# Moving weight sums down VectorE's queue, and using the seven-product form one chunk earlier

## The chip, the cores and the metric

The kernel runs on one core of a Trainium2 chip. The metric is the device time of one execution in microseconds (us); lower is better. The profile of one execution is shown beside the times; its span is about 1.8 us shorter than the time.

Engine names in the profile: PE is TensorE, PEld its weight loads, DVE is VectorE, ACT is ScalarE, POOL is GpSimd (here it only issues loads), SP issues stores.

## The reference, cut to what matters

Attention with projected keys and values, followed by a feed-forward layer with a squared ReLU. There are 8 batches of 1024 tokens, 8 heads of 64.

```python
k_proj = np.einsum('ks,bhsd->bhkd', E, k)         # 64 projected keys per head
v_proj = np.einsum('ks,bhsd->bhkd', F, v)
scores = scale * np.matmul(q, k_proj.transpose(0, 1, 3, 2))
attn = softmax(scores)                            # cut
x = (attn @ v_proj), heads joined: 8192 x 512     # cut
h = np.maximum(x @ w_in, 0.0)                     # 512 -> 2048, the first layer
out = h * h @ w_out                               # 2048 -> 512, the second layer
```

## The kernel before

Each batch is worked in two chunks of 512 tokens. A chunk first does the first layer (16 blocks `fb` of four 512-column products, ReLU on ScalarE into `h_relu`, square on VectorE into `hsq`), then the second layer. The attention of the next batch is put between these steps by a plan: `at(step, ...)` issues a piece behind that step. TensorE's order is as written. The order on the other engines is chosen by a scheduler at build time, and each of them then works strictly in that order.

The second layer of a chunk has two forms. The plain form is 64 products of 512 columns. The other uses seven half-size matrix products in place of eight (112 of 256 columns) and needs eight sums of quarters of `w_out` (once, into `w_sum`) and eight sums of quarters of `hsq` (per chunk, `h_sum`, with one written over `hsq`), all on VectorE.

```python
def sum_w_out():                                  # 8 instructions on VectorE
    for j in range(2):
        ...                                       # quarters of w_out_sb[j], w_out_sb[j + 2]
        for o, x, y in ((t1, b12, b11), (t3, b22, b12), (t2, b22, t1), (t4, b21, t2)):
            nc.vector.tensor_tensor(out=o, in0=x, in1=y, op=ALU.subtract)

def seven_products(self, c):                      # cut
    first, chain, other = bank(), bank(), bank()
    half(c, 1, 0, first, True); yield             # needs the squares of fb 0 to 7
    half(c, 1, 1, first, True)
    nc.scalar.copy(chain[:], first[:]); yield     # ScalarE: starts the chain of product 6
    half(c, 5, 0, other, True); yield             # needs the first h sums
    half(c, 5, 1, other, True); yield
    half(c, 6, 0, chain, False); yield            # ...

def steps(self):                                  # cut
    for c in range(2):
        seven = self.b > 0                        # the first batch uses the plain form
        order = [fb for j in range(HF) for fb in (j, HF + j)] if seven else range(fb0, NFB)
        for n, fb in enumerate(order):
            ...                                   # 4 products, ReLU, square; h sums after n = 7 and 15
            yield

# the plan of the first batch (b == 0), cut
at(1, att.project_v, V_PIECES[1])                 # its own attention still runs in chunk 0
at(2, att.chunk_values, 0, 1, (0,))
at(36, nxt.project)                               # the next batch's attention, in chunk 1
at(39, nxt.transpose_k)
at(45, nxt.sums, 0)
at(48, nxt.values, 0, True)                       # True: into banks of the first layer
at(48, nxt.scores, 2)
...
at(64, sum_w_out)                                 # last in the program
```

PSUM is in two pools: `bank()` turns round four banks used by both layers, and `att_psum()` round two tiles for the attention. Of the attention's tiles, `vp` holds the projected values, `rs` the inverse row sums (VectorE copies part of them to other partitions: the `rs` copies), and `xT` the attention's result, which is the first layer's input.

The softmax here doesn't subtract the row's maximum and nothing guards it: scores larger than these inputs give would overflow.

Of the kernel before, what the change touches and what calls it, by code (L numbers as in the profile page):

```python
# [18 lines left out]
def kernel(  # L19
# [11 lines left out]
    nc = tc.nc  # L31
# [41 lines left out]
    def bank(shape=(P, 512), dtype=F32):  # L73
        return fps.tile(list(shape), dtype, tag="bank", name="ps_bank")
# [61 lines left out]

    w_sum = wpool.tile([P, 4, HF, HM], BF16, name="w_sum")

    def sum_w_out():
        for j in range(2):  # L140
            f = slice(j * fn, (j + 1) * fn)
            t1, t2, t3, t4 = (w_sum[:, n, f] for n in range(4))
            up, down = w_out_sb[j], w_out_sb[j + 2]
            b11, b12, b21, b22 = up[:, :, 0:HM], up[:, :, HM:DM], down[:, :, 0:HM], down[:, :, HM:DM]
            for o, x, y in ((t1, b12, b11), (t3, b22, b12), (t2, b22, t1), (t4, b21, t2)):
                nc.vector.tensor_tensor(out=o, in0=x, in1=y, op=ALU.subtract)
# [34 lines left out]
    class Attention:  # L181
# [58 lines left out]
        def transpose_k(self, gs=(0, 1)):  # L240
            ps = bank([P, H // 2, 2, KP], BF16)
            rows = slice((LO, HI)[gs[0]].start, (LO, HI)[gs[-1]].stop)
            g = slice(gs[0], gs[-1] + 1)
            for j in range(H // 2):
                nc.tensor.transpose(
                    ps[:, j, g, :].rearrange("p g k -> p (g k)"),
                    self.kp[rows, j].rearrange("k a d -> k (a d)"), ident[rows, rows]
                )
            nc.vector.tensor_copy(self.kT[:, :, g], ps[:, :, g])

        def transpose_k_dma(self):
            nc.sync.dma_start_transpose(
# [122 lines left out]
    class Ffn:  # L375
# [113 lines left out]
        def steps(self):  # L489
            for c in range(2):  # L490
                self.hsq[c] = hsq_pool.tile([P, 2, 2, HF, HC], BF16, name="hsq")
                seven = self.b > 0
                if seven:
                    self.h_sum = form_pool.tile([P, 3, HF, HC], BF16, name="h_sum")
                first = self.cold and c == 0
                fb0 = 0
                if first:

                    banks = [bank() for _ in range(4)]
                    for cbs, fbs in (  # L500
                        ((0, 1), (0, 1)), ((0, 1), (2, 3)), ((2,), (0, 1)), ((2,), (2, 3)), ((3,), (0, 1, 2, 3)),
                    ):
                        for fb in fbs:
                            for cb in cbs:
                                self.first_mm(c, fb, cb, banks[fb])
                            if cbs[-1] == NCB - 1:
                                self.square(c, fb, banks[fb])
                        if (cbs, fbs) != ((2,), (2, 3)):
                            yield
                    fb0 = 4  # L510
                order = [fb for j in range(HF) for fb in (j, HF + j)] if seven else range(fb0, NFB)
                for n, fb in enumerate(order):
                    ps = bank()
                    for cb in range(NCB):
                        self.first_mm(c, fb, cb, ps)
                    self.square(c, fb, ps)
                    if seven and n % HF == HF - 1:
                        self.sum_h(c, slice(n // HF * HF // 2, (n // HF + 1) * HF // 2))
                    yield
                if first:  # L520

                    for t0 in range(0, 4, 2):
                        banks = [bank() for _ in range(2)]
                        for j in range(WP):
                            for t in range(2):
                                for fb in range(j * fn, (j + 1) * fn):
                                    self.second_mm(c, t0 + t, fb, banks[t])
                                if j == WP - 1:
                                    self.store(c, t0 + t, banks[t])
                                yield  # L530
                elif seven:
                    yield from self.seven_products(c)
                else:
                    for tb in range(4):
                        ps = bank()
                        for j in range(WP):
                            for fb in range(j * fn, (j + 1) * fn):
                                self.second_mm(c, tb, fb, ps)
                            if j == WP - 1:
                                self.store(c, tb, ps)  # L540
                            yield

    with tc.manual_schedule(engines={PE}):
# [28 lines left out]
        coming = None  # L572
        for b in range(B):
            plan = {}

            def at(step, fn, *args, **kwargs):
                plan.setdefault(step, []).append(lambda: fn(*args, **kwargs))

            if b == 0:
                at(1, att.project_v, V_PIECES[1])  # L580
                at(2, att.chunk_values, 0, 1, (0,))
                at(2, att.project_v, V_PIECES[2])
                at(3, att.chunk_values, 0, 1, (1,))
                at(21, att.transpose_q_chunk, 1, Q0, 0)
                at(21, att.transpose_q_chunk, 1, Q0, 1)
                at(23, att.chunk_scores, 1, 0)
                at(23, att.chunk_scores, 1, 1)
                at(25, att.sums, 0)
                at(27, att.chunk_values, 1, 0)
                at(27, att.chunk_values, 1, 1)  # L590
                nxt = Attention(1)
                nxt.load()
            if b + 1 < B:
                if b + 2 < B:
                    coming = Attention(b + 2)
                    coming.load()
                if b == 0:
                    at(36, nxt.project)
                    at(39, nxt.transpose_q, 0)
                    at(39, nxt.transpose_q, 1)  # L600
                    at(39, nxt.transpose_k)
                    at(41, nxt.scores, 0)
                    at(41, nxt.scores, 1)
                    at(44, nxt.transpose_q, 2)
                    at(44, nxt.transpose_q, 3)
                    at(45, nxt.sums, 0)
                    at(48, nxt.values, 0, True)
                    at(48, nxt.scores, 2)
                    at(51, nxt.values, 1)
                    at(51, nxt.scores, 3)  # L610
                    at(55, nxt.sums, 2)
                    at(55, nxt.values, 2)
                    at(55, nxt.values, 3, True)
                else:
                    at(14, nxt.scores, 0)
                    at(14, nxt.scores, 1)
                    at(18, nxt.sums, 0)
                    at(18, nxt.values, 0)
                    at(21, nxt.scores, 2)
                    at(26, nxt.values, 1)  # L620
                    at(26, nxt.scores, 3)
                    at(48, nxt.sums, 2)
                    at(48, nxt.values, 2)
                    at(51, nxt.values, 3)
                if b + 2 < B:
                    if b == 0:
                        at(61, coming.project)
                        at(63, coming.transpose_q_dma)
                        at(64, coming.transpose_k)
                        at(64, sum_w_out)  # L630
                    else:
                        at(26, coming.project)
                        at(30, coming.transpose_q_dma)
                        at(28, coming.transpose_k_dma)
            for step, _ in enumerate(Ffn(att, b == 0).steps(), 1):
                for stage in plan.pop(step, []):
                    stage()
            assert not plan, plan
            att, nxt = nxt, coming
# [30 lines left out]
```

## Time and profile before

| | before |
|---|---|
| time | 512.07 us (511.62 to 512.73, 3 runs) |
| span of the profile | 510.1 us |
| TensorE busy | 96% of the span |
| VectorE / ScalarE busy | 60% / 55% |

From the second batch on TensorE works almost without a gap. The first batch does not. These are TensorE's longest waits in the kernel before (who waited, for what: us in all, times, longest):

```profile
PE ps_att L296 <- DVE vp L238: 12.4, 2, 11.2
PE ps_bank L471 <- DVE xT L371: 2.0, 3, 1.5
PE ps_bank L410 <- DVE hsq L386: 1.9, 6, 0.3
```

`vp` is the copy of projected values out of PSUM. The copy itself is short, so the question is what it stood behind. This is TensorE's timeline before, from 19 us (start, duration, engine, line, operation; in brackets the idle time in front of it and what ended it):

```profile
20.23 0.64 PE L235 MATMUL ps_att<-V_sb,FT 128*64 128x128 bf16 x16
20.80 1.04 PE L471 MATMUL ps_bank<-xT,w_in 128*128 128x512 bf16 x4
33.08 0.43 PE L296 MATMUL ps_att<-expT,vp 64*64 64x256 bf16 x4 [11.24 <-DVE vp L238]
...
38.49 13.93 PE L471 MATMUL ps_bank<-xT,w_in 128*128 128x512 bf16 x54
52.25 1.03 PE L477 MATMUL ps_bank<-w_out,hsq 128*128 128x512 bf16 x4
```

And VectorE's timeline in the same stretch:

```profile
18.75 0.68 DVE L371 TENSOR_TENSOR xT<-ps_att,rs 128x512 bf16<-128x512 f32 x1
32.13 0.69 DVE L146 TENSOR_TENSOR w_sum<-w_out 128x1024 bf16<-128x1024 bf16 x1 [12.69 <-DMA w_out<-in_moe_w_out_dram]
32.74 0.28 DVE L238 CAST vp<-ps_att 128x128 bf16<-128x128 f32 x1
34.63 0.69 DVE L146 TENSOR_TENSOR w_sum<-w_out 128x1024 bf16<-128x1024 bf16 x1 [1.61 <-DMA w_out<-in_moe_w_out_dram]
35.24 0.68 DVE L371 TENSOR_TENSOR xT<-ps_att,rs 128x512 bf16<-128x512 f32 x1
```

Read the two together. The projection that `vp` copies had ended by 20.9 us, yet the copy ran at 32.74. In front of it stood a sum of `w_out`, whose data landed only at about 32.1. The sum is written last in the program and is not needed before the second batch, but the scheduler placed it here. The Trainium skill (TensorE: Matmul & The Clock Gate, "Architectural detail") says that VectorE's and ScalarE's queues are strict FIFO while TensorE's can only pull weight loads ahead; this trace agrees: nothing overtook the waiting sum for 12.69 us.

The page's strip of the granted TensorE clock (40 slices of 12.75 us, in tenths) shows a second cost:

```profile
PEclk9958999999999999999999999999999999999999
```

The granted clock was 0.51 from 25.5 to 38 us and 0.50 from 38 to 42 us, so the 54 products at 38.49 took longer than the 11.7 us that 54 times 0.216 us make.

### The profile page before, as it was taken

The numbers are of one execution on the slowest core, as the hardware profiler recorded it, in microseconds if no ns is written. First come the engines' busy times: TensorE is split into PE (matmuls) and PEld (weight loads), VectorE is DVE, ScalarE is ACT, GpSimd is POOL, SyncE is SP. The second block draws the span as 40 slices with busy tenths as digits, with TensorE's granted clock in tenths as the row PEclk, the third lists the DMA queues.
The fourth block names the chain that finished last, engine by engine and source line by source line (L and its number), as shares of the span: only waits on it lengthen the run. The fifth ranks groups of instructions, "written<-read, shape, count | busy, mean of one in ns | idle before, by whom it ended". The sixth has DMA issues, their size and how long they took to land.

```text
span 510.1 us, 8489 instructions
## 1 busy us (share of the span) xinstructions
PE 487.1 (96%) x3434; PEld 287.8 (56%) x3434; DVE 304.9 (60%) x586; ACT 282.7 (55%) x425; POOL 32.5 (6%) x45
## 2 busy tenths in 40 slices
PE   8629999999999999999999999999999999999996
PEld 4214444445657465665748465574747566575755
DVE  2226266667666675857667665756767574757271
ACT  2306447547464775647465675747665575745351
POOL 7420010010100002000100000000000000000000
PEclk9958999999999999999999999999999999999999
DMA  9999999994697009920499106020330202020202
GB/s 174 204 204 207 208 209 181 198 202 81 136 192 158 21 1 220 203 83 1 93 172 198 47 1 175 2 84 0 91 86 1 82 2 84 0 84 1 82 2 84
DMA packets 74905, 54.30 MB, mean 106 GB/s; under 512 B 29169, under 2 KB 73457, under 8 KB 74865
## 3 DMA queue, kind: packets, MB, share of 16 engines
q0 software_dynamic: 30640, 29.23, 36.1%
q1 hardware_dynamic: 44224, 24.52, 18.3%
q8 instruction: 27, 0.44, 0.3%
q14 instruction: 14, 0.11, 0.1%
HBM read 59.24 MB, written 16.78 MB: 149 GB/s over the span
## 4 chain that ended last, share of the span: by engine, by line
PE 86%; DMA 6%; issue 3%; ACT 3%; DVE 1%; POOL 1%; POOLq 0%
PE ps_bank L471 41%; PE ps_bank L410 33%; PE ps_bank L477 4%; DMA w_out<-in_moe_w_out_dram 3%; DMA V_sb<-in_v_dram 3%; PE ps_bank L215 2%; PE ps_att L342 2%; ACT h_relu L384 1%; PE ps_att L320 1%; PE ps_att L286 1%; ACT expT L300 1%; DVE hsq L386 1%; DVE xT L371 0%; PE ps_bank L271 0%; POOL K_sb L80 0%
## 5 line engine op out<-in xcount | busy, mean ns | idle before, releaser
L471 PE MATMUL ps_bank<-xT,w_in 128*128 128x512 bf16 x1024 | 228.8, 382 | 2.1 <-DVE xT L371 2.0
L384 ACT ACTIVATE h_relu<-ps_bank 128x512 bf16<-128x512 f32 x256 | 151.8, 599 | 107.9 <-PE ps_bank L471 107.7
L471 PEld LDWEIGHTS <-w_in 128*128 128x128 bf16 x1024 | 99.6, 98 | 122.8 <-issue 9.7
L386 DVE TENSOR_TENSOR hsq<-h_relu 128x512 bf16<-128x512 bf16 x256 | 105.8, 423 | 90.0 <-ACT h_relu L384 89.1
L410 PEld LDWEIGHTS <-hsq 128*128 128x128 bf16 x896 | 86.6, 98 | 19.0 <-DVE hsq L386 3.6
L410 PEld LDWEIGHTS <-h_sum 128*128 128x128 bf16 x672 | 63.8, 98 | 12.5 <-issue 5.5
L410 PE MATMUL ps_bank<-w_out,hsq 128*128 128x256 bf16 x448 | 56.8, 273 | 1.9 <-DVE hsq L386 1.9
L410 PE MATMUL ps_bank<-w_sum,hsq 128*128 128x256 bf16 x448 | 53.5, 273 | 0.0
L410 PE MATMUL ps_bank<-w_sum,h_sum 128*128 128x256 bf16 x448 | 53.4, 273 | 0.0
L330 DVE COPY rs<-rs 32x1024 f32<-32x1024 f32 x60 | 41.1, 685 | 20.3 <-ACT rs L325 19.4
L420 DVE TENSOR_TENSOR o_sb<-ps_bank,u 128x512 f32<-128x512 f32 x28 | 19.4, 691 | 46.9 <-PE ps_bank L410 30.4
L428 ACT COPY u<-ps_bank 128x512 f32<-128x512 f32 x28 | 16.4, 585 | 39.9 <-PE ps_bank L410 39.9
L300 ACT ACTIVATE expT<-ps_att 128x1024 bf16<-128x1024 f32 x32 | 31.9, 1025 | 2.7 <-PE ps_att L286 2.6
L346 DVE TENSOR_TENSOR xT<-ps_att,rs 128x512 bf16<-128x512 f32 x52 | 33.0, 685 | 0.5
L477 PE MATMUL ps_bank<-w_out,hsq 128*128 128x512 bf16 x128 | 29.2, 380 | 0.0
L410 PE MATMUL ps_bank<-w_out,h_sum 128*128 128x256 bf16 x224 | 26.7, 273 | 0.0
L418 ACT COPY o_sb<-ps_bank 128x512 f32<-128x512 f32 x28 | 16.4, 585 | 14.3 <-PE ps_bank L410 14.1
L477 PEld LDWEIGHTS <-hsq 128*128 128x128 bf16 x128 | 11.9, 98 | 15.5 <-issue 1.9
L398 DVE TENSOR_TENSOR h_sum<-hsq 128x1024 bf16<-128x1024 bf16 x28 | 19.4, 692 | 1.0
L398 DVE TENSOR_TENSOR h_sum<-h_sum,hsq 128x1024 bf16<-128x1024 bf16 x28 | 19.3, 689 | 0.5
L398 DVE TENSOR_TENSOR h_sum<-hsq,h_sum 128x1024 bf16<-128x1024 bf16 x28 | 19.2, 684 | 0.0
L398 DVE TENSOR_TENSOR hsq<-hsq 128x1024 bf16<-128x1024 bf16 x28 | 19.2, 684 | 0.0
(71 smaller groups left out, 256.0 us busy)
## 6 DMA issues: line engine op xcount, KB each, us to landing
out_dram<-o_sb SPq DMA_DIRECT2D x64, 256.0 KB, 2.3
K_sb<-in_k_dram POOLq DMA_DIRECT2D x7, 1024.0 KB, 14.2
V_sb<-in_v_dram POOLq DMA_DIRECT2D x7, 1024.0 KB, 19.4
Q_sb<-in_q_dram POOLq DMA_DIRECT2D x7, 1024.0 KB, 15.2
w_out<-in_moe_w_out_dram POOLq DMA_DIRECT2D x4, 512.0 KB, 17.0
w_in<-in_moe_w_in_dram POOLq DMA_DIRECT2D x3, 512.0 KB, 14.7
k_f<-in_k_dram SPq DMA_DIRECT2D x1, 512.0 KB, 4.3
Q_sb<-in_q_dram POOLq DMA_DIRECT2D x2, 256.0 KB, 7.8
```

The costliest lines, as they stand in the source:

```text
L300: nc.scalar.activation(e[:], ps[:], AF.Exp, scale=SCALE)
L330: nc.vector.tensor_copy(rs[j][lack:lack + 32], rs[j][have:have + 32])
L346: nc.vector.tensor_tensor(out=self.xT[:, pr, :, par], in0=ps_x[par].rearrange("p (c t) -> p c t", c=2), in1=rs[:, par].rearrange("p (c t) ...
L384: nc.scalar.activation(r[:], ps[:], AF.Relu)
L386: nc.vector.tensor_tensor(out=self.hsq[c][:, fb // HF, :, fb % HF, :], in0=rv, in1=rv, op=ALU.mult)
L398: nc.vector.tensor_tensor(out=o, in0=x, in1=y, op=op)
L410: nc.tensor.matmul(ps[:, i * HM:(i + 1) * HM], lhsT=h[:, fb, i * P:(i + 1) * P], rhs=w_out_form(n, fb), start=fresh and i == 0 and fb == 0 ...
L418: nc.scalar.copy(o[:], ps[:])
L420: nc.vector.tensor_tensor(out=o[:], in0=ps[:], in1=more[:], op=ALU.add)
L428: nc.scalar.copy(u[:], ps[:])
L471: nc.tensor.matmul(ps[:], lhsT=w_in_blk(cb, fb), rhs=self.xT[:, cb, c].rearrange("p a t -> p (a t)"), start=(cb == 0), stop=(cb == NCB - 1),)
L477: nc.tensor.matmul(ps[:, m], lhsT=self.quarter(c, fb // HF, tb // 2)[:, fb % HF, (tb % 2) * P:(tb % 2 + 1) * P], rhs=w_out_blk(fb)[:, m], ...
```

## The change

Its intent has three parts: queue the sums of `w_out` later on VectorE; with the sums in hand, use the seven products in the first batch's second chunk too; and in batches 1 to 6 put the next batch's row sums and values ahead of the seven products. `tc.issue_after(x)` makes the scheduler queue what stands inside it behind instruction `x`; here that is the copy of the next batch's `kT`.

```diff
-    def sum_w_out():
+    def sum_w_out(behind):
+        with tc.issue_after(behind.queued.ins):
+            sum_w_out_now()
+
+    def sum_w_out_now():
...
-            nc.vector.tensor_copy(self.kT[:, :, g], ps[:, :, g])
+            self.queued = nc.vector.tensor_copy(self.kT[:, :, g], ps[:, :, g])
...
-                seven = self.b > 0
+                seven = self.b > 0 or c > 0
...                                                # first batch
+                    at(46, sum_w_out, nxt)
-                    at(55, nxt.values, 3, True)
+                    at(57, nxt.values, 3)
...                                                # later batches
-                    at(14, nxt.scores, 0)          # and scores 1
-                    at(18, nxt.sums, 0)            # and values 0
-                    at(21, nxt.scores, 2)
+                    at(12, nxt.scores, 0)
+                    at(16, nxt.sums, 0)
+                    at(20, nxt.scores, 2)
-                    at(48, nxt.sums, 2)            # and values 2
-                    at(51, nxt.values, 3)
+                    at(46, nxt.sums, 2)
+                    at(50, nxt.values, 3)
...                                                # first batch: 62 steps now, not 64
-                        at(61, coming.project)
-                        at(63, coming.transpose_q_dma)
-                        at(64, coming.transpose_k)
-                        at(64, sum_w_out)
+                        at(59, coming.project)
+                        at(61, coming.transpose_q_dma)
+                        at(62, coming.transpose_k)
```

(The last hunks are shortened; `and ...` comments stand for lines that move alike.)

More of the change, by code (lines that the diff above doesn't have):

```diff
@@ L612 @@
                     at(55, nxt.values, 2)
-                    at(55, nxt.values, 3, True)
+                    at(57, nxt.values, 3)
                 else:
-                    at(14, nxt.scores, 0)
-                    at(14, nxt.scores, 1)
-                    at(18, nxt.sums, 0)
-                    at(18, nxt.values, 0)
-                    at(21, nxt.scores, 2)
+                    at(12, nxt.scores, 0)
+                    at(12, nxt.scores, 1)
+                    at(16, nxt.sums, 0)
+                    at(16, nxt.values, 0)
+                    at(20, nxt.scores, 2)
                     at(26, nxt.values, 1)
                     at(26, nxt.scores, 3)
-                    at(48, nxt.sums, 2)
-                    at(48, nxt.values, 2)
-                    at(51, nxt.values, 3)
+                    at(46, nxt.sums, 2)
+                    at(46, nxt.values, 2)
+                    at(50, nxt.values, 3)
                 if b + 2 < B:
                     if b == 0:
-                        at(61, coming.project)
-                        at(63, coming.transpose_q_dma)
-                        at(64, coming.transpose_k)
-                        at(64, sum_w_out)
+                        at(59, coming.project)
+                        at(61, coming.transpose_q_dma)
+                        at(62, coming.transpose_k)
                     else:
```

## The prediction

> **What bounds the kernel.** TensorE: busy 96% of a 510.1 us span; from the second batch on a batch takes 58.0 us, 57.7 of them TensorE (table by stage). Its waits lie in the first 40 us: the waits view has 12.4 us for VectorE's `vp` copy, 11.2 in one wait. The timeline: VectorE's queue is in order, and a `vp` copy of a product that ended near 20.9 us runs at 32.74, behind a sum of `w_out` that waited 12.69 us for the first `w_out` piece. The next copies wait for pieces landing near 34.6 and 37.2 us. Then the granted clock is 0.51 (25.5 to 38 us) and 0.50 (38 to 42). The Trainium skill (TensorE: Matmul & The Clock Gate, Part 1) says an idle window halves the clock; the trace agrees.
>
> **Sums moved.** `vp` is then copied near 21 us. The waits of the DMA queue put the last V piece at 22.1 us and `w_in` pieces at 24.7, 27.2, 29.8: in time. 54 products at 0.216 us put the first second-layer product at about 36 us instead of 52.25. `w_out` lands at 32.1, 34.6, 37.2 and 42.4 us, just ahead of use. Gain: 16 us, 2 of them clock. The next batch's K, V and Q (landed by about 53 and 58 us) stay ahead of their use at about 57 and 61.
>
> **Seven products in the first batch's second chunk.** 64 products of 512 columns at 0.2225 us (14.2 us) become 112 of 256 at 0.109 (12.25): 2.0 us less.
>
> **Added there on VectorE.** Eight sums of `w_out` and eight of `h`, 0.61 us each: 9.8 us, on 24.8 us busy in 37.5. In the changed order all eight sums of `w_out`, four `h` sums and four `rs` copies (0.7 us) stand before the fifteenth square, which the first of the seven products needs. Summed from the `kT` copy (79.49 us in the old trace), it ends near 93.5; TensorE wants it at 89.6: 4 us of wait, 0.7 more for the second `h` sums, and 1 us at the last product, whose bank waits for an output sum behind the late `xT` products. I expect 5.7 us of new wait: the stage gets 3.7 us longer, not 2 shorter.
>
> **Sums and values ahead of the products (batches 1 to 6).** They fill the wait for the last squares (1.9 us in six waits). ScalarE now does Ln and two Exp (3.2 us) before the copy that starts the third product's chain; it should end about when TensorE comes (0 to 0.3 us per chunk). Net 1.5 us gained.
>
> **Sum.** 512.1 - 16.0 - 2.0 + 5.7 - 1.5 = 498.3 us; 8 in 10 between 493.5 and 502.5. Faster by over 2% (under 501.8): 0.87; within 2%: 0.12; slower: 0.01.
>
> **Right if:** no wait for `vp` over 1 us, clock 1.0 between 20 and 52 us, first second-layer product near 36 us, next projection near 57. In the first batch's second chunk waits of TensorE for `hsq`, `h_sum` or `xT` of 3 to 8 us, VectorE over 85% busy there. 112 more 256-wide products, 64 fewer 512-wide. Later batches: no wait for `hsq`, 57.7 us each.
>
> **Wrong if:** loads land later once TensorE is early (a DMA wait near 22, 42 or 57 us); less waiting in the second chunk (down to 492 us), or more, with a clock that falls again (up to 505); ScalarE's chain copy late in all twelve later chunks (up to 7 us).

## The result

The changed kernel takes 499.27 us (498.89 to 499.96, 4 runs); the kernel before, with the run beside it, 512.32 us. The ratio is 0.9748 (95% interval 0.9731 to 0.9765). All outputs are right. Ratios here are the mean time of one kernel's fast runs over that of the other's of the same rounds, so they are not quite the ratio of the medians quoted.

TensorE's waits after (lines of the changed kernel are four higher, so L414 is the old L410):

```profile
PE ps_bank L414 <- DVE hsq L390: 3.6, 1, 3.6
...
PE ps_bank L475 <- DVE xT L375: 1.1, 4, 0.3
...
PE ps_bank L414 <- DVE o_sb L424: 0.5, 1, 0.5
PE ps_bank L414 <- ACT u L432: 0.3, 1, 0.3
```

The wait for `vp` is gone, and so are the six waits for `hsq` of the later batches; one new wait of 3.6 us has come. TensorE's timeline after, the start of the first batch:

```profile
21.78 0.64 PE L239 MATMUL ps_att<-V_sb,FT 128*64 128x128 bf16 x16
22.35 1.04 PE L475 MATMUL ps_bank<-xT,w_in 128*128 128x512 bf16 x4
23.32 0.30 PE L300 MATMUL ps_att<-expT,vp 64*64 64x256 bf16 x4
...
26.11 11.58 PE L475 MATMUL ps_bank<-xT,w_in 128*128 128x512 bf16 x51 [0.26 <-DVE xT L375]
37.53 4.48 PE L481 MATMUL ps_bank<-w_out,hsq 128*128 128x512 bf16 x20
```

VectorE's timeline after, in the same stretch:

```profile
22.46 0.29 DVE L242 CAST vp<-ps_att 128x128 bf16<-128x128 f32 x1 [1.47 <-PE ps_att L239]
23.74 0.69 DVE L375 TENSOR_TENSOR xT<-ps_att,rs 128x512 bf16<-128x512 f32 x1 [0.99 <-PE ps_att L300]
24.35 0.28 DVE L242 CAST vp<-ps_att 128x128 bf16<-128x128 f32 x1
```

The `vp` copy now runs as soon as its product has ended, the products of the values follow at once, and the second layer starts at 37.53 us in place of 52.25. The granted clock was 1.00 from 20 to 52 us. In the page's strip (slices of 12.45 us here) the first 8 lies before this stretch, and the second, in the seventh slice, belongs to the new wait:

```profile
PEclk8999998999999999999999999999999999999999
```

Now the same kernel's timeline where the new wait is, the start of the seven products in the first batch's second chunk:

```profile
74.07 0.94 PE L414 MATMUL ps_bank<-w_out,hsq 128*128 128x256 bf16 x7
78.65 1.67 PE L414 MATMUL ps_bank<-w_out,hsq 128*128 128x256 bf16 x9 [3.65 <-DVE hsq L390]
80.19 1.87 PE L414 MATMUL ps_bank<-w_sum,h_sum 128*128 128x256 bf16 x8
```

Seven products run, using the squares of `fb` 0 to 6; the eighth needs `fb` 7, the fifteenth square in this order. VectorE's timeline shows what it stood behind:

```profile
72.52 0.68 DVE L150 TENSOR_TENSOR w_sum<-w_out,w_sum 128x1024 bf16<-128x1024 bf16 x1
73.12 0.68 DVE L150 TENSOR_TENSOR w_sum<-w_out 128x1024 bf16<-128x1024 bf16 x1
73.72 0.42 DVE L390 TENSOR_TENSOR hsq<-h_relu 128x512 bf16<-128x512 bf16 x1
74.06 0.68 DVE L150 TENSOR_TENSOR w_sum<-w_out,w_out 128x1024 bf16<-128x1024 bf16 x1
74.75 2.78 DVE L334 COPY rs<-rs 32x1024 f32<-32x1024 f32 x4
77.56 0.69 DVE L150 TENSOR_TENSOR w_sum<-w_out,w_sum 128x1024 bf16<-128x1024 bf16 x1
78.17 0.42 DVE L390 TENSOR_TENSOR hsq<-h_relu 128x512 bf16<-128x512 bf16 x1
```

No line has an idle time: VectorE is working through a backlog. The square that TensorE waits for is the one at 78.17.

The stages of both kernels, in us, from the timelines (a boundary is the first product of a layer):

| stage | before | after | difference |
|---|---|---|---|
| start to the first product of the first layer | 18.89 | 20.44 | +1.55 |
| first batch, chunk 0, first layer | 33.36 | 17.09 | -16.27 |
| first batch, chunk 0, second layer | 16.67 | 16.66 | 0 |
| first batch, chunk 1 | 37.53 | 42.76 | +5.23 |
| batches 1 to 6 | 347.41 | 344.63 | -2.78 |
| batch 7 | 56.24 | 56.21 | -0.03 |
| span | 510.1 | 497.8 | -12.3 |

The trace of the changed kernel lacks some matmul records (992 of the first layer's 1024 are there), among them the first product of batches 2 to 7. The table puts these starts one product (0.22 us) before the first record; the complete traces of other runs with the moved steps give the same 344.6 us.

The first row is not the change's: over twelve profiles that stage took 18.59 to 21.46 us, with no relation to the kernel (the same source gave 20.44 and 18.66). The kernel before absorbs a late start in its wait and the changed kernel does not, so the first two rows belong together: -14.7 us (worked out below). A profile's span is therefore a poor measure of 1 us; the timed runs decide there.

### The profile page after: what moved, and what is told of

The parts are those of the page before. It is cut to its first block, busy times and chain, and to the rows that moved or that the text cites. A ratio compares the mean times of both kernels' runs of the same rounds, so it can differ in the third digit from the quotient of the medians.

```text
span 497.8 us, 8559 instructions
## 1 busy us (share of the span) xinstructions
PE 482.8 (97%) x3446; PEld 293.4 (59%) x3482; DVE 310.9 (62%) x596; ACT 281.6 (57%) x426; POOL 32.5 (7%) x45
## 4 chain that ended last, share of the span: by engine, by line
PE 89%; DVE 6%; ACT 2%; issue 1%; DMA 1%; DVEq 0%; POOLq 0%
PE ps_bank L475 42%; PE ps_bank L414 37%; PE ps_bank L219 2%; PE ps_att L346 2%; PE ps_att L290 2%; DMA K_sb<-in_k_dram 1%; DVE rs L334 1%; PE ps_bank L481 1%; DVE xT L375 1%; PE ps_att L324 1%; DVE w_sum L150 1%; DVE hsq L390 1%; PE ps_bank L228 1%; PE ps_bank L179 1%; DVE qT L279 1%
## 5 line engine op out<-in xcount | busy, mean ns | idle before, releaser
L475 PE MATMUL ps_bank<-xT,w_in 128*128 128x512 bf16 x992 | 223.3, 379 | 3.0 <-DVE xT L375 1.1
L414 PEld LDWEIGHTS <-hsq 128*128 128x128 bf16 x960 | 92.1, 98 | 22.1 <-issue 6.9
L414 PEld LDWEIGHTS <-h_sum 128*128 128x128 bf16 x720 | 69.8, 98 | 12.4 <-issue 4.1
L414 PE MATMUL ps_bank<-w_out,hsq 128*128 128x256 bf16 x480 | 60.6, 274 | 3.6 <-DVE hsq L390 3.6
L414 PE MATMUL ps_bank<-w_sum,h_sum 128*128 128x256 bf16 x480 | 57.9, 275 | 0.0
L414 PE MATMUL ps_bank<-w_sum,hsq 128*128 128x256 bf16 x480 | 57.5, 272 | 0.3 <-ACT u L432 0.3
L424 DVE TENSOR_TENSOR o_sb<-ps_bank,u 128x512 f32<-128x512 f32 x30 | 20.7, 691 | 55.9 <-PE ps_bank L414 30.9
L414 PE MATMUL ps_bank<-w_out,h_sum 128*128 128x256 bf16 x240 | 28.6, 273 | 0.5 <-DVE o_sb L424 0.5
L80 POOL DMA_DIRECT2D K_sb<-in_k_dram x9 | 7.8, 861 | 138.5 <-PE ps_bank L220 134.1
L330 ACT ACTIVATE rs<-rs 128x1024 f32<-128x1024 f32 x15 | 15.9, 1062 | 0.5
## 6 DMA issues: line engine op xcount, KB each, us to landing
w_out<-in_moe_w_out_dram POOLq DMA_DIRECT2D x4, 512.0 KB, 17.8
w_in<-in_moe_w_in_dram POOLq DMA_DIRECT2D x3, 512.0 KB, 14.7
k_f<-in_k_dram SPq DMA_DIRECT2D x1, 512.0 KB, 4.3
```

Of the source, the lines that this page charges most:

```text
L330: nc.scalar.activation(rs[1][:], rs[1][:], AF.Exp, scale=-1.0)
L414: nc.tensor.matmul(ps[:, i * HM:(i + 1) * HM], lhsT=h[:, fb, i * P:(i + 1) * P], rhs=w_out_form(n, fb), start=fresh and i == 0 and fb == 0 ...
L424: nc.vector.tensor_tensor(out=o[:], in0=ps[:], in1=more[:], op=ALU.add)
L475: nc.tensor.matmul(ps[:], lhsT=w_in_blk(cb, fb), rhs=self.xT[:, cb, c].rearrange("p a t -> p (a t)"), start=(cb == 0), stop=(cb == NCB - 1),)
```

## The experiments

All ran with rounds of the kernel before on the same chip, whose medians were 511.6 to 512.0 us. My theory had three parts: (1) the early sums, by holding VectorE's queue, were the whole of the first gap; (2) the sums standing among the squares make the new wait; (3) the moved steps shorten the later batches. The rivals were that the seven products carry part of the gain, that the `h` sums and not the sums of `w_out` make the new wait, and that batches 1 to 6 are shorter for another reason.

### One part at a time

**Sums of `w_out` only** (`e1_sums_only`): the two hunks of `sum_w_out` and `self.queued`, `at(46, sum_w_out, nxt)`, and nothing else.

```diff
-    def sum_w_out():
+    def sum_w_out(behind):
+        with tc.issue_after(behind.queued.ins):
...
+                    at(46, sum_w_out, nxt)
...
-                        at(64, sum_w_out)
```

> Only the sums of w_out move on VectorE (queued as in the changed kernel); no seven products in the first batch's second chunk, no step moves. Theory (the early sums hold VectorE's queue, and nothing else was needed): the first second-layer product starts 16.3 us earlier than before, and the second chunk of the first batch keeps its 37.5 us, because without the products' sums the late squares are still in time: 496.0 us, so faster than the changed kernel (499.3). Rival (the seven products are part of the gain, and the wait in the second chunk comes from the sums of w_out alone): a wait of some 4 us stays in the second chunk and the time is 500 to 503 us.

Measured: 496.74 us (496.08 to 496.87), ratio 0.9708 (0.9691 to 0.9724). Chunk 0's first layer fell to 17.08 us and chunk 1 kept its 37.54; the second layer began at 37.18 us, so 15.1 us earlier and not 16.3 (why is said under the first gap below). The theory holds, and one part of the change alone beats the whole.

**Seven products only** (`e2_seven_only`): the sums stay where the scheduler put them. By my notes, a first build read `w_sum` before it was written, since the sums stood behind their use in the program; it was never run. The run has `at(46, sum_w_out)` instead, and its trace shows the scheduler still hoisting the sums to the front (the first at 32.19 us).

```diff
-                seven = self.b > 0
+                seven = self.b > 0 or c > 0
...
+                    at(46, sum_w_out)
...                                                # and the first batch's steps 57, 59, 61, 62
```

> Only the seven products in the first batch's second chunk (with that batch's own step numbers, which the shorter chunk forces); the sums of w_out stay early in VectorE's queue. The 12.4 us of waits for vp must stay. Theory: TensorE has 2.0 us less to do there, and the h sums alone make it wait about 1.7 us (fifteenth square 0.5, second h sums 1.2): 511.5 to 512.5 us, the second chunk 37.2 us long instead of 37.5. Rival (the wait of 3.65 us comes from the h sums or the rs copies, not from the sums of w_out): the chunk gets as long as in the changed kernel, 42.8 us, and the time is 517 us.

Measured: 513.81 us (513.41 to 514.79), ratio 1.0049 (1.0034 to 1.0064): slower than before, a small but clear difference. Chunk 1 took 39.86 us, so 2.7 us more than I expected and 2.9 less than in the changed kernel. Neither side was right: the sums of `w_out` cost about 2.9 us of the 42.8, and the seven products lose on their own.

**Steps of batches 1 to 6 only** (`e3_steps_only`):

```diff
-                    at(18, nxt.sums, 0)            # and 14, 21, 48, 51, as in the change
+                    at(16, nxt.sums, 0)            # and 12, 20, 46, 50
```

> Only the moved steps of batches 1 to 6 (sums and values ahead of the products). Theory: each of these batches gets 0.46 us shorter (58.21 to 57.75), 2.8 us in all: 509.5 us. Rival (the shorter batches of the changed kernel have another cause, such as the loads being further ahead): no change, 512.3 us.

Measured: 509.29 us (508.98 to 509.46), ratio 0.9957 (0.9942 to 0.9972). Batches 1 to 6 took 344.64 us in place of 347.40. The theory holds. The start of the seven products in batch 1, in the kernel before and in this run:

```profile
120.93 0.93 PE L410 MATMUL ps_bank<-w_out,hsq 128*128 128x256 bf16 x7
122.17 1.16 PE L410 MATMUL ps_bank<-w_out,hsq 128*128 128x256 bf16 x9 [0.32 <-DVE hsq L386]
```

```profile
121.95 1.92 PE L410 MATMUL ps_bank<-w_out,hsq 128*128 128x256 bf16 x16
```

The row sums and values stand before the products now, and the sixteen run without a break.

### The sums where VectorE is idle

**Sums in the gap** (`e4_sums_in_gap`): VectorE was idle for 5.95 us in chunk 0's second layer, after the `qT` copies, and all of `w_out` has landed by then.

```diff
-            nc.vector.tensor_copy(self.qT[:, 4 * hg:4 * hg + 4, 2 * c:2 * c + 2, :], ps[:])
+            self.queued = nc.vector.tensor_copy(self.qT[:, 4 * hg:4 * hg + 4, 2 * c:2 * c + 2, :], ps[:])
...
-                    at(46, sum_w_out, nxt)
+                at(21, sum_w_out, att)
```

> The changed kernel with the sums of w_out queued behind the two qT copies of the first batch's chunk 1, where VectorE was idle for 5.95 us (43.8 to 49.7 us in the changed kernel); eight sums take 4.9 us. Theory (the wait of 3.65 us, the half clock after it and the two small waits come from the sums standing among the squares): the second chunk of the first batch falls from 42.8 to about 37.2 us (1.7 us of wait for the h sums left) and the time to 493.8 us. Rival (h sums and rs copies are to blame): the wait stays at 3 us or more and the time at 499 us.

Measured: 496.13 us (495.60 to 496.99), ratio 0.9702. Chunk 1 took 39.58 us. The long wait went, so the sums among the squares were its main cause, but the chunk is 2.4 us longer than I expected. TensorE's waits of this run:

```profile
PE ps_bank L414 <- DVE xT L350: 1.3, 1, 1.3
...
PE ps_bank L414 <- DVE o_sb L424: 0.5, 1, 0.5
PE ps_bank L414 <- DVE hsq L390: 0.4, 1, 0.4
PE ps_bank L414 <- ACT u L432: 0.3, 1, 0.3
```

These add up to 2.5 us. TensorE's timeline shows that a wait costs more than this view lists:

```profile
74.12 0.94 PE L414 MATMUL ps_bank<-w_out,hsq 128*128 128x256 bf16 x7
75.50 1.16 PE L414 MATMUL ps_bank<-w_out,hsq 128*128 128x256 bf16 x9 [0.44 <-DVE hsq L390]
77.97 1.22 PE L414 MATMUL ps_bank<-w_sum,h_sum 128*128 128x256 bf16 x8 [1.31 <-DVE xT L350]
```

At 0.109 us each, the product after seven would have started at 74.88; it started at 75.50. That is 0.62 us lost where 0.44 is listed, because a product's listed end (0.27 us after its start) lies 0.16 us beyond the start of its successor in a full pipeline. The second wait is for `other`: in the rotation of four banks it is a bank that the next batch's values used, and it comes free only when VectorE has done the `xT` products behind the `rs` copies.

### The clock after the wait

**Idle products in the wait** (`f2_warm_wait`), beside **the changed kernel again** (`f1_changed_again`):

```diff
+    def warm_att(n):
+        ps = att_psum()
+        for _ in range(n):
+            nc.tensor.matmul(ps[:, 0, :], lhsT=zeros[:, 0:P], rhs=zeros[:], start=True, stop=True)
...
+                    at(48, warm_att, 16)
```

> The changed kernel once more, as the measure for the three runs beside it: 499.3 us.

> The changed kernel with 16 idle products of 512 columns (zeros, into a free bank of the attention; 3.46 us) put into TensorE's wait for the fifteenth square, which lasts 3.8 us. VectorE's and ScalarE's order is the same. Theory: the wait stays, but the clock stays at full speed, so that the 17 products after it take 0.11 us each and not 0.17 to 0.22: the second chunk of the first batch is 1.0 to 1.5 us shorter, 498.0 us. Rival (the slow products after the wait wait for h sums, not for the clock): no change, 499.3 us.

Measured: 499.06 us (498.23 to 499.22) for the changed kernel, 498.01 us (497.48 to 498.24) with the idle products; the ratios to before are 0.9741 (0.9728 to 0.9755) and 0.9725 (0.9711 to 0.9738), so the intervals overlap; the slowest run with the idle products (498.24) is level with the fastest without them (498.23). Chunk 1 took 43.64 us without and 41.86 us with them. The profile of the run with them (the added lines shift line numbers: L419 is the changed kernel's L414):

```profile
73.46 3.63 PE L185 MATMUL ps_att<-zeros 128*128 128x512 bf16 x15
76.92 0.93 PE L419 MATMUL ps_bank<-w_out,hsq 128*128 128x256 bf16 x7
78.05 1.16 PE L419 MATMUL ps_bank<-w_out,hsq 128*128 128x256 bf16 x9 [0.20 <-DVE hsq L395]
79.58 1.21 PE L419 MATMUL ps_bank<-w_sum,h_sum 128*128 128x256 bf16 x8 [0.38 <-DVE xT L355]
```

The nine products took 1.16 us, in place of 1.67 in the first profile of the changed kernel, and 2.10 in the second:

```profile
77.42 2.10 PE L414 MATMUL ps_bank<-w_out,hsq 128*128 128x256 bf16 x9 [3.65 <-DVE hsq L390]
```

The granted clock over the chunk was 1.00; in the second profile of the changed kernel it was 0.50 from 77 to 82.5 us. So some 0.9 to 1.8 us of the stage were the half clock that follows the wait, and work without use, costing nothing while TensorE waits, took it away. The small wait for `xT` is in neither waits list of the changed kernel; probably it was hidden under the slow products and came out when these got fast.

### Putting the parts together

**Sums and steps, no seven products in the first batch** (`f3_sums_and_steps`, run twice, the second time as `g2_sums_and_steps_again`): `e1_sums_only` plus the steps of batches 1 to 6. Against the changed kernel:

```diff
-                seven = self.b > 0 or c > 0
+                seven = self.b > 0
...                                                # first batch's steps back to 55, 61, 63, 64
```

> The changed kernel's two gains without its loss: sums of w_out late, steps of batches 1 to 6 moved, no seven products in the first batch. If the parts add (sums only 496.7, steps 2.3 to 2.8): 494.1 us, faster than before and than the changed kernel. If the steps' gain overlaps with the sums' gain: 496.5 us.

> Sums late and steps moved, without seven products in the first batch, once more beside the run above: 493.0 us.

Measured: 493.03 us (492.98 to 493.84), ratio 0.9633 (0.9619 to 0.9646), beside the changed kernel's 499.06; and 493.30 us, ratio 0.9641, in the second call. The parts add, and this version beats both kernels. It is even about 1 us below the 494.1 us that the single parts add up to; its two profiles started early (18.61 and 18.59 us, `e1_sums_only` at 20.10), which may be why. Chunk 1 took 37.54 and 37.55 us. TensorE's longest waits in the first of these runs, which are all from before the second chunk:

```profile
PE ps_bank L179 <- DVE zeros L111: 1.2, 1, 1.2
PE ps_bank L475 <- DVE xT L375: 1.1, 4, 0.3
PE ps_bank L170 <- DVE e_bf L549: 0.8, 1, 0.8
```

**Can the seven products pay here at all?** Two more placements with the sums in the gap. In `f4_gap_shift` the next batch's attention comes two steps earlier (the first transposes and scores one). In `g1_gap_shift_42` its first values also go into an attention bank, behind the last square:

```diff
-                    at(36, nxt.project)            # and 39, 41, 44: transposes, scores
-                    at(45, nxt.sums, 0)
-                    at(48, nxt.values, 0, True)
-                    at(48, nxt.scores, 2)
+                    at(34, nxt.project)            # and 38, 40, 42
+                    at(42, nxt.sums, 0)            # f4: 43
+                    at(46, nxt.scores, 2)
+                    at(48, nxt.values, 0)          # f4: at(46, nxt.values, 0, True)
```

> Sums in the gap with the seven products, and the next batch's attention in the first batch two steps (1.7 us) earlier, the first q transposes and scores one step, so that rs copies and xT products come before the last squares. In the run with the sums in the gap, waits with their pipeline drains cost about 3.5 us in the second chunk (other bank held by xT 1.5, square 0.6, output sum 0.7, u copy 0.5, h sums 0.3). Theory (only these waits keep the seven products from paying 2 us): 492.6 to 493.5 us, below sums and steps alone. Rival (the seven products cannot pay in a chunk that also carries a whole attention): 495 us or more. K and V of the next batch land at 48 and 54 us and Q at 61, so a wait of up to 0.5 us for Q is possible.

> Sums in the gap with the seven products, the next batch's attention earlier as in the last run, its first row sums one step earlier still, and its first values one to two steps later and in a bank of the attention, so that neither rs copies nor values hold the last squares or the banks of the first layer. The last run lost about 3 us of waits in the second chunk (banks of the first layer 1.1, square 1.2, rest 0.7) and came out 2.3 us above sums and steps alone. If the waits go, the chunk takes 36.0 to 36.5 us instead of 38.6 and the time is 493.0 us, a tie with sums and steps alone; below 492 us the seven products would pay after all.

Measured: 495.33 us (494.87 to 495.38), ratio 0.9672, and 494.76 us (493.98 to 496.02), ratio 0.9665. Chunk 1 took 38.62 and 37.92 us, against 37.54 for the plain form. The first met the rival's figure (495 us or more). The second was 1.5 us above the plain form's 493.30, not a tie, though its profile has a late start of 21.46 us and its chunk 1 is only 0.4 us longer. In five placements (42.8, 39.9, 39.6, 38.6, 37.9 us) the seven products never came below the plain form, though they have less work for TensorE: 1.6 us less, by the starts in these traces (64 products 0.216 us apart against 112 that are 0.109 apart). What is left in the last one is only partly named: its waits list shows 0.9 us for an `xT` product that holds an attention tile and 0.2 us for ScalarE's `u` copy, and the rest is spread over small gaps in the timeline. That no placement could pay is not shown.

## Why the prediction was right, point by point

- **The total** was 498.3 us; measured were 499.27 us, inside the range.
- **The first gap, 16.0 us**: the stage table has 16.27, but the changed kernel also started 1.55 us later, and the kernel before would have absorbed that. With the early sums the second layer began at 52.25, 51.95 and 52.50 us in three profiles (before, `e2_seven_only`, `e3_steps_only`) whose first layer began at 18.89, 20.32 and 19.86: there the wait ends when `w_out` lands (first sum at 32.13, 32.19 and 31.85). So the gain of this pair of profiles is 52.25 - 37.53 = 14.7 us, and the single part gave 14.9 us of time (511.61 to 496.74). The forecast held for a start as early as 18.89: the repeat of the changed kernel, which started at 18.66, had its second layer at 35.84, and then lost 0.46 us in that layer, where a wait of 0.30 us for `w_out` is listed. The trace showed each step named: `vp` is copied within 0.2 us of its product's end, the clock is 1.00 from 20 to 52 us, the second layer starts at 37.53 us (36 plus the late start of 1.55), and after the start no wait for loads of over 0.3 us is listed in the profiles with the sums moved.
- **Seven products, 2.0 us less, 5.7 us new wait, net +3.7**: the sign and the place were right, the size was not. Chunk 1 grew by 5.23 us in one profile and 6.11 in the other. The wait for the fifteenth square was as summed (3.8 us lost between the products, 4 forecast). The wait at the last product came where it was forecast, for the output sum behind the late `xT` products (0.69 us lost, 1 forecast); none for the second `h` sums (0.7) is listed. Two things were mis-sized. The saving is 1.6 us and not 2.0: the 512-column products start 0.216 us apart in the trace before, not 0.2225. And missing from the sum was the half clock behind the wait (0.9 us in this profile), which the prediction listed under what would make it wrong but set at zero.
- **VectorE's load there**: 20.8 of 24.4 us busy up to the end of the wait, 85%; the forecast of "over 85%" was right only for that part.
- **Steps of batches 1 to 6, 1.5 us**: 2.78 in the profile, 2.3 in the time of the single part. The waits for `hsq` went, as forecast; ScalarE's chain copy was never waited for. Each of these batches got 0.46 us shorter. The wait was listed at 0.32 us, but a wait costs more than its listed length: in the timeline before, seven products from 120.93 us at 0.109 us each reach 121.69, and the eighth started at 122.17, 0.48 us later. I had summed the listed lengths, and took something off for ScalarE.
- **A reading of mine that was off**: "a batch takes 58.0 us" was the length of the windows that I had chosen. The starts of the batches lie 58.21 us apart before and 57.75 after.

Three terms were mis-sized, by the profiles: the first gap by 1.3 us too much gain, the seven products by 1.5 too little loss, the steps by 1.3 too little gain. The last made up for most of one of the others, so that the total came within 1 us is in part luck. A right total is no proof of its terms: the prediction saw that the seven products would lose here, but only the run of the single part showed that the other two parts alone are 6 us faster (493.03 to 499.06).

## What to carry to other kernels

Where a scheduler orders a strictly ordered engine, look for instructions that it placed long before their result is needed: one that waits for a late load blocks all that stand behind it. When such work would land among work that is waited for, put it where that engine's timeline shows an idle stretch, not merely later. And a form with less work for the bottleneck engine can lose where its helpers have no room; before a change of several parts is kept, run each part alone.

## What the Trainium skill lacked or had wrong

- TensorE: Matmul & The Clock Gate, "Part 1", says that one idle window of about 3.4 us brings the half clock. The trace agrees: after a listed wait of 3.65 us the clock was 0.50, after waits of 1.3 us it stayed at full speed. Under "Terms" the page puts the penalty at about the throttled time times one half at this clock, which came out too high here. The half clock lasted 3.4 us in one profile of the changed kernel and 6.8 in the other, so 1.7 and 3.4 us by that rule (an estimate), and against the run with idle products (41.86) chunk 1 was 0.9 and 1.8 us longer (42.76 and 43.64); in 1.5 of the 6.8 us TensorE was still in its wait. It warns of idle gaps of over about 3 us; that idle products inside a wait keep the clock up for free is not said there (42.76 and 43.64 to 41.86 us in the chunk, 499.06 to 498.01 us of time).
- The same page, "Back-to-back issue gap", gives about 131 ns per product of 512 columns for a sustained stream of weight loads and products. Here 64 such pairs took 13.8 us, 216 ns each, in every later batch, which is the page's figure for the isolated gap; 256 columns took 109 ns, as its formula for the isolated gap has it.
- No page that I read says how much a list of waits leaves out: a wait is counted from the listed end of the last product, and in a full pipeline of 256-column products the loss was about 0.18 us more than the wait listed (0.62 lost, 0.44 listed).
